# Longformer attention and a softplus feed-forward block on one core: global rows picked 512 columns at a time, the first q load cut by sequence, and the instruction order rebuilt

## The chip, the cores and the metric

The kernel runs on one core of one Trainium2 chip, in one launch. The metric is the device time in microseconds. A profiled execution gives the span from the first to the last instruction and the events inside it.

## The reference

The kernel fuses two functions. The first is attention with a window of 32 on both sides and eight global positions; the second is a feed-forward block with softplus.

```python
# q, k, v: [8 batches, 8 heads, 576 rows, 64]; global_idx: 8 rows
scores = (1 / np.sqrt(64)) * np.matmul(q, k.transpose(0, 1, 3, 2))
mask = np.abs(pos[:, None] - pos[None, :]) <= 32
mask = mask | is_global[:, None] | is_global[None, :]
attn = softmax(np.where(mask, scores, -1e9))
attn_out = np.matmul(attn, v)
x = attn_out.transpose(0, 2, 1, 3).reshape(8 * 576, 512)
h = x @ w_in                          # [4608, 512] @ [512, 2048]
g = np.maximum(h, 0.0) + np.log1p(np.exp(-np.abs(h)))
out = g @ w_out                       # [4608, 2048] @ [2048, 512]
```

## The kernel before

Each batch of 576 rows is cut into nine blocks of 64 rows; a unit is one such block with all eight heads, so there are 72 units. Four units are a group of 256 tokens, and two groups make a tile of 512 tokens for the feed-forward block; there are eight tiles.

Preparation of a batch (add_prep): one load brings q and one brings k (load_qk, L224), 72 partitions with eight sequence rows each, all heads. TensorE transposes them (tk L499, tq L507; 16 products of 72 columns for a pair of heads), and copies of ScalarE or VectorE put them into kx and qx. The rows of the eight global positions are picked by products with a 0/1 matrix pick_w (pick, L456): for each of q and k, eight products over the rows in a partition, for each of four pairs of heads, 128 columns each. Each pair of heads has its own quarter of the output's partitions. A copy (keep) brings the result to gk, a transposition (turn, L468) gives gt, and from there fill writes the global keys beside every window in kx, and gev writes the global queries to qg.

Scores of a unit come in two halves of four heads (sc, L621, and L626 in the first batch). VectorE adds the mask and finds the row's extreme (top, L632). ScalarE takes the exponentials (ex, L653). VectorE sums and inverts (su, L661 to L663). GpSimd scales: no (pn, L669) for the window and gc (gw, L673) for the global columns. The scaled block is transposed by TensorE (tp, L679) and copied (pt), or transposed by a DMA. The global rows have a part of their own: sg L548, gexp L561, tg L575, ov L586, oz L590. For four units together rt (L712) and val (xo, L734 and L744) give the attention output, which xev copies to xT.

The feed-forward block of a tile: first (h, L778) makes 16 groups of four products, soft (L784) takes softplus on ScalarE, second (o, L789) makes 16 products for each 128 tokens, and oev copies and stores. The first tile runs its first product in two halves of 256 tokens.

In the first batch q and k are loaded in two halves of four heads: k, q, then, after the constants are made, k, q again, all from GpSimd's queue. Blanks, the five loads of v and the two loads of w_in follow in that queue.

The order of all instructions is written out ahead of time by a planner in the kernel itself (class _Order). Each piece of work is added with a cost for each engine that can do it, its dependences, a rank, and the PSUM banks and buffers that it opens. run() takes, at each step, the piece that can start first, with the rank to break ties, and gives it to an engine. The engines then run their queues in that order. Ranks are shifted by two tables, OPENING for the early pieces and LATER for the others; KINDS says how many PSUM banks each kind of result may hold.

```python
    KINDS = dict(h=(4, 1), o=(2, 1), s=(2, 1), pick=(1, 2), gt=(1, 1), tk=(1, 2), tq=(4, 2), tk0=(2, 0), tq0=(2, 0),
                 sg=(2, 1), tg=(1, 0), ov=(1, 0), tp=(3, 0), rt=(3, 0), xo=(4, 2))
    OPENING = dict(ex=-1.5, gexp=-2, gsum=2.5, pt=2.5, softh=2, su=2, top=-2, w_out=-2)
    LATER = dict(blank_g=-1, blank_q=0.5, first=1, kev=-7, load=1, re=2, sg=2, soft=3, su=-0.5, tk=-5.5, tp=-1)
```

Of the kernel before, what the change touches and what calls it, by code (L numbers as in the profile page):

```python
# [18 lines left out]
class _Order:  # L19
# [15 lines left out]
    SWITCH = 95  # L35

# [41 lines left out]
    def run(self, free):  # L78
        waiting = {}
        after = {}  # L80
# [11 lines left out]
        while ready:  # L92
# [23 lines left out]
            step, took = j["cost"][e]  # L116
            for pool, key in j["opens"]:
# [9 lines left out]
            if e == "PE" and j["array"] != array:  # L127
                array = j["array"]
                t += self.SWITCH
            if j["moves"]:  # L130
# [24 lines left out]
def kernel(  # L155
# [71 lines left out]

    def load_v(b, t):
# [13 lines left out]
    load_qk(0, 0, 0, H // 2)  # L242
# [20 lines left out]
    for h in range(2):  # L263
# [3 lines left out]
    count(posA[:], [[P, NT5]], -WIN, 1)  # L267
    pick_w = const([P, QR, 32], BF16, "pick")
    clear(nc.vector, pick_w[:])
    nc.vector.tensor_tensor(out=pick_w[:, :, 0:NG], in0=posQ[:].unsqueeze(2).to_broadcast([P, QR, NG]),  # L270
                            in1=gf[:].unsqueeze(1).to_broadcast([P, QR, NG]), op=OP.is_equal)
# [22 lines left out]
    selg = const([P, 2, 2], FP32, "selg")  # L294
    hsel = temp([P, 2], FP32, "hsel")
# [5 lines left out]
    load_qk(0, 1, H // 2, H)  # L301
    load_qk(0, 0, H // 2, H)
# [56 lines left out]

    def select_rows():  # L360
# [17 lines left out]
    for c in range(KF):  # L378
        SLOTS[f"g{c}"] = 1

    KINDS = dict(h=(4, 1), o=(2, 1), s=(2, 1), pick=(1, 2), gt=(1, 1), tk=(1, 2), tq=(4, 2), tk0=(2, 0), tq0=(2, 0),
                 sg=(2, 1), tg=(1, 0), ov=(1, 0), tp=(3, 0), rt=(3, 0), xo=(4, 2))
# [24 lines left out]
    def pool(n):  # L407
        return {"POOL": (n, n)}
# [11 lines left out]
    def add_load(b, which, deps):  # L420
# [6 lines left out]
        early = [T.get(("t" + "qk"[which], b - 1, p)) for p in range(HP)]  # L427
# [12 lines left out]
    def add_prep(b, gate, rank):  # L440
# [8 lines left out]
        def pick(e, ws):  # L449
            if ("pick", b) not in PS:  # L450
                PS["pick", b] = psum(("pick", b), [P, 2, 2 * P], FP32)
                PS["gk", b] = sb.tile([P, 2, P], BF16, tag="gk", name="gk")
            for w in ws:
                for r in range(QR):
                    for p in range(HP):
                        nc.tensor.matmul(out=PS["pick", b][p * 32:(p + 1) * 32, w, 0:P], lhsT=pick_w[0:NQ, r, :],  # L456
                                         rhs=XN[w][0:NQ, p * 2:p * 2 + 2, r * D:(r + 1) * D],
                                         start=(r == 0), stop=(r == QR - 1))

        def keep(e, ws):  # L460
            r = slice(ws[0], ws[-1] + 1)
            copy(e, PS["gk", b][:, r, :], PS["pick", b][:, r, 0:P])

        def turn(e, ws):
            if ("gt", b) not in PS:
                PS["gt", b] = psum(("gt", b), [P, 2, HP, 32], BF16)
            for w in ws:
                nc.tensor.transpose(out=PS["gt", b][:, w, :, :], in_=PS["gk", b][:, w, :], identity=ident_b[:])  # L468
# [9 lines left out]
        steps = ((1,), (0,)) if b == 0 else ((0, 1),)  # L478
        for n, ws in enumerate(steps):
            T["pick", b, n] = o.add({"PE": (1040, 1160) if b == 0 else (460 * len(ws) + 190, 460 * len(ws) + 300)}, lambda e, ws=ws: pick(e, ws),  # L480
                                    [x for w in ws for x in T["load", b, w]] + [T.get(("pick", b, n - 1)), *gate], rank=4 if b or not n else 6, array=32,
                                    opens=[("pick", ("pick", b)), ("gk", ("gk", b))] if n == 0 else [],
                                    uses=[("pick", b), ("gk", b)])
# [51 lines left out]
        if b == 0:  # L535
            T["pick", 0, 1]["deps"] += [T["tq", 0, p] for p in range(2, HP)]
# [458 lines left out]
```

## Time and profile before

| | us |
|---|---|
| three runs, median (lowest to highest) | 375.19 (372.39 to 376.84) |
| profiled execution, its time | 370.3 |
| profiled execution, span of the core | 368.5 |
| TensorE busy | 342.6 (93%) |
| ScalarE busy | 277.5 (75%) |
| VectorE busy | 230.8 (63%) |
| GpSimd busy | 153.5 (42%) |

In the profile PE is TensorE's product, PEld its weight load, DVE is VectorE, ACT ScalarE, POOL GpSimd, SP SyncE. In the lists of instructions a line has the start and the time that it took in us, the engine, the source line, the operation, output and inputs, the shape, and a count; the bracket gives the idle time of the engine ahead of it and what ended it. "issue" means that the engine waited for nothing that the profile shows. Single products overlap, so the time per product is the distance of starts, not the time from start to end.

### The profile page before, as it was taken

What the parts mean: (1) busy time and instruction counts of PE and PEld (TensorE: products, weight loads), DVE (VectorE), ACT (ScalarE), POOL (GpSimd) and SP (SyncE); (2) the same over time, 40 slices, a digit from 0 to 9 for tenths busy, and PEclk for the clock granted to TensorE, in tenths of its full rate; (3) what the DMA queues carried; (4) which work ended last, traced back from release to release, by engine and by line L of the source; (5) the groups of instructions that cost most, each with busy time, mean ns of one, the idle gap of its engine ahead of it and who ended that gap; (6) DMA issues with size and microseconds to landing.
All of it is one profiled execution on the core that took longest, in us unless ns stands there. A gap on an engine that the chain in (4) does not pass through costs nothing.

```text
span 368.5 us, 11196 instructions
## 1 busy us (share of the span) xinstructions
PE 342.6 (93%) x4265; PEld 196.8 (53%) x4308; DVE 230.8 (63%) x1028; ACT 277.5 (75%) x709; POOL 153.5 (42%) x256
## 2 busy tenths in 40 slices
PE   2858999999999999899989999999999999999996
PEld 2646794565556454654464445554554455445444
DVE  5788796876588539854885568666965584163011
ACT  4598879986799679876978598859885996774710
POOL 8999712870079006910592049302930271050000
PEclk9999999999999999999999999999999999999999
DMA  6999993499049933993269516971691022021002
GB/s 92 171 221 162 179 216 57 99 97 189 15 116 136 184 65 98 123 202 64 86 117 174 106 46 133 165 142 45 129 138 45 31 86 59 0 74 59 0 29 85
DMA packets 86165, 39.01 MB, mean 106 GB/s; under 512 B 68064, under 2 KB 79584, under 8 KB 86112
## 3 DMA queue, kind: packets, MB, share of 16 engines
q0 software_dynamic: 53248, 18.37, 46.9%
q1 hardware_dynamic: 32864, 19.94, 22.2%
q8 instruction: 33, 0.54, 0.6%
q14 instruction: 20, 0.16, 0.1%
HBM read 36.71 MB, written 9.44 MB: 125 GB/s over the span
## 4 chain that ended last, share of the span: by engine, by line
PE 77%; DVE 10%; issue 4%; ACT 4%; POOL 3%; DMA 2%; DVEq 0%; POOLq 0%; ACTq 0%
PE h L778 33%; PE o L789 23%; PE s L621 4%; DVE sm L661 3%; PE xo L744 3%; PE pick L456 2%; PE tk L499 2%; PE tq L507 2%; PE tp L679 2%; DMA qn<-in_q_dram 2%; PE xo L734 2%; DVE st L632 2%; POOL pn L669 1%; ACT pe L653 1%; DVE rs L663 1%
## 5 line engine op out<-in xcount | busy, mean ns | idle before, releaser
L669 POOL TENSOR_TENSOR pn<-pe,rs 128x512 bf16<-128x512 f32 x72 | 74.8, 1039 | 173.2 <-DVE rs L663 136.2
L778 PE MATMUL h<-xT,win 128*128 128x512 bf16 (+1 forms) x625 | 135.8, 358 | 1.1 <-PE s L621 0.4
L789 PE MATMUL o<-wout,g 128*128 128x512 bf16 (+1 forms) x564 | 128.6, 373 | 2.0 <-issue 1.3
L784 ACT ACTIVATE g<-h 128x512 bf16<-128x512 f32 (+1 forms) x160 | 86.7, 555 | 45.5 <-PE h L778 44.4
L632 DVE CUSTOM_DVE_ANT_0 st<-s,mask 128x136 f32<-128x136 f32 x288 | 69.5, 296 | 47.7 <-PE s L621 45.0
L653 ACT ACTIVATE pe<-st,nb 128x136 f32<-128x136 f32 x288 | 92.5, 403 | 0.0
L778 PEld LDWEIGHTS <-win 128*128 128x128 bf16 x640 | 59.3, 98 | 50.5 <-issue 2.5
L789 PEld LDWEIGHTS <-g 128*128 128x128 bf16 x592 | 55.4, 98 | 55.4 <-DMA kn<-in_k_dram 0.3
L661 DVE TENSOR_REDUCE sm<-pe 128x4 f32<-128x544 f32 x63 | 44.7, 710 | 10.9 <-ACT pe L653 10.7
L231 POOL DMA_DIRECT2D vA<-in_v_dram x40 | 34.4, 875 | 0.0
L414 DVE COPY osb<-o 128x512 f32<-128x512 f32 (+1 forms) x21 | 13.8, 659 | 28.6 <-PE o L789 28.6
L621 PEld LDWEIGHTS <-qx 128*128 128x128 bf16 x252 | 20.6, 98 | 13.7
L621 PE MATMUL s<-kx,qx 128*128 128x136 bf16 x252 | 27.0, 223 | 0.4
L414 DVE COPY qx<-tq 64x576 bf16<-64x576 bf16 (+1 forms) x28 | 21.1, 753 | 4.7 <-PE tq L507 4.3
L632 DVE DVE_READ_ACCUMULATOR2_ANT nb<- 128x1 f32 x288 | 23.8, 83 | 0.0
L499 PE MATMUL tk<-ident_b,kn 72*64 72x72 bf16 x512 | 14.7, 207 | 7.6 <-DMA kn<-in_k_dram 7.3
L414 ACT COPY qx<-tq 64x576 bf16<-64x576 bf16 (+1 forms) x32 | 20.4, 637 | 0.9 <-PE tq L507 0.7
L663 DVE TENSOR_TENSOR rs<-rs,notg 128x4 f32<-128x4 f32 x72 | 17.7, 246 | 2.7 <-DVE rs L662 0.2
L414 ACT COPY kx<-tk 128x32 bf16<-128x32 bf16 (+1 forms) x63 | 15.9, 329 | 4.4 <-PE tk L499 4.3
L499 PEld LDWEIGHTS <-kn 72*64 72x64 bf16 x512 | 11.5, 118 | 11.7 <-DMA kn<-in_k_dram 7.5
L673 POOL TENSOR_TENSOR gw<-pe,rs 128x32 bf16<-128x32 f32 x72 | 16.8, 238 | 0.0
L662 DVE RECIPROCAL rs<-sm 128x4 f32<-128x4 f32 x72 | 12.7, 177 | 6.5
(110 smaller groups left out, 337.3 us busy)
## 6 DMA issues: line engine op xcount, KB each, us to landing
out_dram<-osb SPq DMA_DIRECT2D x35, 256.0 KB, 2.2
vB<-vA SPq DMA_DIRECT2D x16, 256.0 KB, 7.0
kn<-in_k_dram POOLq DMA_DIRECT2D x7, 576.0 KB, 12.5
qn<-in_q_dram POOLq DMA_DIRECT2D x7, 576.0 KB, 15.2
vA<-in_v_dram POOLq DMA_DIRECT2D x24, 128.0 KB, 6.1
win<-in_moe_w_in_dram POOLq DMA_DIRECT2D x2, 1024.0 KB, 13.8
wout<-in_moe_w_out_dram POOLq DMA_DIRECT2D x4, 512.0 KB, 10.2
vA<-in_v_dram POOLq DMA_DIRECT2D x16, 96.0 KB, 5.1
```

The costliest lines, as they stand in the source:

```text
L231: nc.gpsimd.dma_start(out=vA[b % 2][p0:p0 + hi - lo, t, :].rearrange("p (h d) -> p h d", h=H), in_=SRC[2][b, :, lo:hi, :].rearrange("h s d ...
L414: (nc.scalar.copy if e == "ACT" else nc.vector.tensor_copy)(out, in_)
L499: nc.tensor.transpose(out=ps[h * D:(h + 1) * D, r, :], in_=kn[0:NQ, p * 2 + h, r * D:(r + 1) * D], identity=ident_b[0:NQ, 0:NQ])
L621: nc.tensor.matmul(out=ps[:, y, :], lhsT=qx[i][:, p, j, :, :].rearrange("c h q -> c (h q)"), rhs=kf[:, p, j * W:j * W + EXT], start=True, ...
L632: nc.vector.tensor_tensor_reduce(out=PS["st", n][:, p, :], in0=PS["s", n, x][:, y, :], in1=mask[:, j, :], scale=-SCALE, scalar=3.0e38, op0 ...
L653: nc.scalar.activation(out=pe[:, p, 0:EXT], in_=PS["st", n][:, p, :], func=AF.Exp, bias=PS["nb", n][:, p:p + 1], scale=-1.0, **({"accum_ou ...
L661: nc.vector.reduce_sum(out=sm[:], in_=PS["pe", n][:, :, 0:EXT], axis=AX)
L663: nc.vector.tensor_tensor(out=rs[:], in0=rs[:], in1=notg[:, j:j + 1].to_broadcast([P, HP]), op=OP.mult)
L669: nc.gpsimd.tensor_tensor(out=pn[:].rearrange("c p (a s) -> c p a s", a=2), in0=wide[:, :, :, 0:G], in1=rs[:].unsqueeze(2).unsqueeze(3).to ...
L778: nc.tensor.matmul(out=h[:, :], lhsT=w_in_t[c * P // WC][:, kd, c * P % WC:c * P % WC + P], rhs=PS["xT", m][:, kd, lo:hi], start=(kd == 0) ...
L784: nc.scalar.activation(out=PS["g", m, c][:, lo:hi], in_=PS[key][:, :], func=AF.Softplus)
L789: nc.tensor.matmul(out=PS[key][:, :], lhsT=PS["g", m, kf][:, ns * P:(ns + 1) * P], rhs=w_out_t[kf // 4][:, kf % 4, lo:hi], start=(kf == 0) ...
```

## The change

It has four parts.

- The pick of a batch takes all eight heads in one product of 512 columns. The eight rows r of a partition are spread over the four quarters of the output's partitions (r and r + 4 accumulate), so there are eight products for q and eight for k in place of 64. The copy to gk is 512 columns for each of q and k, and the transposition becomes four products for each with sel8, a 0/1 matrix that adds up the four quarters; gt is f32 now. q and k are separate pieces in every batch.
- The first batch's k comes in two halves of heads, both ahead of the constants. Its q comes in two parts of the sequence, 32 and 40 of the 72 partitions, all heads: Q_PARTS puts the second at partition 64. Its transposes (tq and a new tqb), copies and pick are done part by part. pick_0 is a second 0/1 matrix for these places.
- The planner counts TensorE's instructions (many) and adds waits for the fetch of each 256; it doubles TensorE's costs until 3 us after the first values block.
- KINDS and the rank tables have new values, and a rank can be set for a single piece.

```diff
+    WARM = 3000
+    ASKS, HOLDS, COMES = 170, 448, 3600
...
+            if j.get("warms"):
+                self.cold = t + self.WARM
+            if e == "PE" and t < self.cold:
+                step, took = 2 * step, 2 * took
...
+            if e == "PE":
+                many = j.get("many", 2)
+                for x in range(issued, issued + many):
+                    if x % 256 == self.ASKS:
+                        block[x // 256] = t + (x - issued) * step / many + self.COMES
+                    if x % 256 == self.HOLDS % 256 and x >= self.HOLDS:
+                        late = block[(x - self.HOLDS) // 256] - (t + (x - issued) * step / many)
+                        step, took = step + max(0, late), took + max(0, late)
+                issued += many
...
+    Q_PARTS = ((0, 0, 32), (32, G, NQ - 32))
...
-    load_qk(0, 0, 0, H // 2)
+    load_qk(0, 1, H // 2, H)
...
-    load_qk(0, 1, H // 2, H)
-    load_qk(0, 0, H // 2, H)
+    for lo, at, n in Q_PARTS:
+        nc.gpsimd.dma_start(out=qn[at:at + n, :, :],
+                            in_=q[0].rearrange("h (q r) d -> q h (r d)", r=QR)[lo:lo + n])
...
+    def make_sel8():
+        sel8f = temp([P, NG], FP32, "sel8f")
+        nc.vector.reduce_sum(out=sel8f[:], in_=ident[:].rearrange("p (a r) -> p r a", r=32)[:, 0:NG, :], axis=AX)
+        nc.vector.tensor_copy(sel8[:], sel8f[:])
...
-    KINDS = dict(h=(4, 1), o=(2, 1), s=(2, 1), pick=(1, 2), gt=(1, 1), tk=(1, 2), tq=(4, 2), tk0=(2, 0), tq0=(2, 0),
-                 sg=(2, 1), tg=(1, 0), ov=(1, 0), tp=(3, 0), rt=(3, 0), xo=(4, 2))
+    KINDS = dict(h=(4, 2), o=(3, 1), s=(2, 0), pick=(2, 0), gt=(1, 2), tk=(4, 0), tq=(4, 2), tk0=(1, 0), tq0=(2, 0),
+                 sg=(2, 1), tg=(2, 1), ov=(1, 1), tp=(2, 0), rt=(3, 0), xo=(4, 1))
...
-        def pick(e, ws):
...
-            for w in ws:
+            ps = PS["pick", b, w] = psum(("pick", b, w), [P, H, D], FP32)
+            parts = ((pick_w, 0, NQ),) if b or w else tuple((pick_0, at, n) for lo, at, n in Q_PARTS)
+            for z, (pw, at, n) in enumerate(parts):
                 for r in range(QR):
-                    for p in range(HP):
-                        nc.tensor.matmul(out=PS["pick", b][p * 32:(p + 1) * 32, w, 0:P], lhsT=pick_w[0:NQ, r, :],
-                                         rhs=XN[w][0:NQ, p * 2:p * 2 + 2, r * D:(r + 1) * D],
-                                         start=(r == 0), stop=(r == QR - 1))
+                    c = r % 4 * 32
+                    nc.tensor.matmul(out=ps[c:c + 32, :, :], lhsT=pw[at:at + n, r, :],
+                                     rhs=XN[w][at:at + n, :, r * D:(r + 1) * D],
+                                     start=(r < 4 and z == 0), stop=(r > 3 and z == len(parts) - 1))
...
-                nc.tensor.transpose(out=PS["gt", b][:, w, :, :], in_=PS["gk", b][:, w, :], identity=ident_b[:])
+            for p in range(HP):
+                nc.tensor.matmul(out=PS["gt", b][:, w, p, :], lhsT=PS["gk", b][:, w, p * P:(p + 1) * P], rhs=sel8[:, :],
+                                 start=True, stop=True)
...
-        steps = ((1,), (0,)) if b == 0 else ((0, 1),)
+        for n, w in enumerate((1, 0)):
...
+            def tq(e, z=0, p=p, parts=parts):
+                lo, at, n = parts[z]
+                ps = PS["tq", b, p, z] = psum(("tq", b, p, z), [P, QR, n], BF16)
                 for r in range(QR):
                     for h in range(2):
                         nc.tensor.transpose(out=ps[h * D:(h + 1) * D, r, :],
-                                            in_=qn[0:NQ, p * 2 + h, r * D:(r + 1) * D],
-                                            identity=ident_b[0:NQ, 0:NQ])
+                                            in_=qn[at:at + n, p * 2 + h, r * D:(r + 1) * D],
+                                            identity=ident_b[at:at + n, at:at + n])
...
-    OPENING = dict(ex=-1.5, gexp=-2, gsum=2.5, pt=2.5, softh=2, su=2, top=-2, w_out=-2)
-    LATER = dict(blank_g=-1, blank_q=0.5, first=1, kev=-7, load=1, re=2, sg=2, soft=3, su=-0.5, tk=-5.5, tp=-1)
+    OPENING = dict(blank_w=-2, first=0.5, no=0.5, oev=2, ones_g=-2, sec=4.5, su=2.5, w_in=1, w_out=-4)
+    LATER = dict(first=2, gc=-1, kev=-8, oev=-0.5, pick=2, qev=1, re=2, sec=1, sg=3, su=1.5, top=-0.5, w_out=-4)
```

The resulting order of the opening differs as follows. TensorE takes a k group, the k pick, k, two q groups of the first part, gt, k, two more q groups, the first halves of units 0 and 1, k, two q groups of the second part, the first halves of units 2 and 3, the last two q groups, the second half of unit 0, the q pick, and then the other scores. On GpSimd the four loads of w_out go ahead of pn of units 5 to 8, gw goes ahead of pn in the first eight units, and the two memsets of the mask's ends come behind the five loads of v. On ScalarE the copies pt of units 4 and 5 stand between the exponentials of units 6, 7 and 8. In later batches q and k transposes, the two picks and the values block stand in another order, and the first tile's scores of batch 1 come in the second half of its h groups instead of through both.

## The prediction

> **What bounds the kernel now.** I read the table of busy time in four stretches first, because the whole-span shares mix a start-up with a long steady part.
>
> ```profile
> core 0: us, PE busy (x) PEld busy (x) DVE busy (x) ACT busy (x) POOL busy (x), PEclk, DMA share, GB/s
> ...
> 16.30:34.00 17.70, 12.39 (x172) 8.79 (x169) 15.79 (x102) 15.99 (x78) 16.07 (x33) 1.00 1.11 201
> 34.00:368.50 334.50, 322.06 (x3888) 181.20 (x3929) 205.61 (x882) 254.35 (x613) 122.85 (x186) 1.00 0.65 100
> ```
>
> The first long product (h, L778) starts at 34.00. From there TensorE is busy 322.1 of 334.5 us while VectorE (DVE) has 61% and ScalarE (ACT) 76%. So after 34 only TensorE work and TensorE gaps count. Between 16.3 and 34, ACT, DVE and POOL are all at about 90% and TensorE is not: the chain of exponentials (L653) sets the time there.
>
> Then the timeline of TensorE around the global-row products (pick, L456):
>
> ```profile
> 39.98 1.21 PE L507 MATMUL tq<-ident_b,qn 72*64 72x72 bf16 x64
> 41.02 0.43 PE L499 MATMUL tk<-ident_b,kn 72*64 72x72 bf16 x16
> 41.38 0.51 PE L456 MATMUL pick<-qn,pick 72*32 72x128 bf16 x21
> 42.69 0.35 PE L456 MATMUL pick<-qn,pick 72*32 72x128 bf16 x11 [0.80 <-issue]
> ```
>
> A run of equal products stops for 0.80 us with nothing that releases it ("issue"). Such stops stand at instructions 1210, 2234, 4278, 5046, 5300, 6068 and 7088 of TensorE's order: 176 to 186 past a multiple of 256, each time. The queue table explains the 256:
>
> ```profile
> q8 instruction: 33, 0.54, 0.6%
> ```
>
> 33 packets of 16 KB carry TensorE's 8618 instructions, 256 each. TensorE ran out of instructions. Start to start, less the normal spacing, the seven cost 1.0 + 0.56 + 0.74 + 0.99 + 0.53 + 0.60 + 0.50 = 4.9 us. The 0.25 us "issue" ahead of most other picks is not such a stop: the order has a 512-column product (0.22 us) there which the trace did not record.
>
> Last the opening, TensorE and ACT:
>
> ```profile
> 8.19 1.17 PE L507 MATMUL tq<-ident_b,qn 72*64 72x72 bf16 x32 [0.52 <-DMA qn<-in_q_dram]
> 10.18 1.17 PE L499 MATMUL tk<-ident_b,kn 72*64 72x72 bf16 x32 [0.82 <-DMA kn<-in_k_dram]
> 11.28 1.04 PE L456 MATMUL pick<-kn,pick 72*32 72x128 bf16 x32
> 12.62 1.17 PE L507 MATMUL tq<-ident_b,qn 72*64 72x72 bf16 x32 [0.29 <-DMA qn<-in_q_dram]
> ```
>
> ```profile
> 16.28 0.41 ACT L653 ACTIVATE pe<-st,nb 128x136 f32<-128x136 f32 x1
> ...
> 33.26 1.14 ACT L414 COPY pt<-tp 128x512 bf16<-128x512 bf16 x2 [1.69 <-PE tp L679]
> 34.42 1.28 ACT L784 ACT_TABLE_LOAD   x1
> 35.71 0.38 ACT L784 ACTIVATE g<-h 128x256 bf16<-128x256 f32 x1
> ```
>
> The reader sees when the four loads land (6.5, 8.2, 10.2, 12.6) and that 32 transposes take 1.10 here (10.18 to 11.28) but 64 take 1.04 at 40: TensorE runs at half rate before 34, though the granted-clock column says 1.00. Exponentials start at 16.28; softplus starts at 35.71 and frees the h banks.
>
> **The change, part by part, from 368.5 us of span.**
>
> *Instructions.* Pick goes from 64 to 16 products per batch, each with its weight load: 96 fewer, 768 in eight batches. The second transposition of the picked rows (gt, L468) grows from 2 to 8 products, and the first batch has 64 more transposes and 8 more pick products. 8618 becomes 8090. I added row prices along both orders, from 170 past a multiple of 256 to the need 272 later. In the old order this gives 2.4 to 2.9 us at five of the seven stops, 3.6 at 41.9, over 5 at 195.7 (its packet came late, behind another stop), and 3.1 at one place that did not stop. In the new order the shortest spans after the opening are 3.4, 3.5, 3.5, 3.6, 3.7 and 4.3. At the short stops the instructions were there 3.2 to 3.6 us after the asking place, so I take 4.9 - 0.2 = 4.7 us saved. Bounds: 4.9 saved, and 0.7 lost if every fetch takes the 4.6 us of the one at 41.9 (1.2 + 1.1 + 1.1 + 1.0 + 0.9 + 0.3 = 5.6 us of stops instead of 4.9).
>
> The Trainium skill, Runtime: NRT & Kernel Launch, section Instruction fetch mechanics, also has 16 KiB blocks of 256 instructions, but says that the fetch is hidden because issue is slower than refill. By that the stops have another cause and nothing of the 4.7 is sure; the seven places above speak against it.
>
> *Pick products.* Old: 227.63 to 228.64, 1.01 us for 64. New: four rounds of 512 columns; the eight sg products (L548; 384 and 256 columns, four column places at once) took 0.39 with one 0.1 change of array shape, 0.45 ns a column, so 2048 columns make 0.92 + 0.1. Gain 0 to 0.04 a batch; I take 0.3 in all, with one array change less here and there.
>
> *Eight gt products.* Width 8, weights 128 wide. Bounds from rows: 16 ns each (L744, 64-wide weights) and 59 (L621, 128-wide, 136 columns). They keep the wide weights and lose the columns, so 45: 0.36 - 0.11 = +0.25 a batch, +1.7 us in the seven later batches (0 to +2.5).
>
> *Copies.* Two of 128x512 f32 (0.58 on ACT, 0.68 on DVE, row xT<-xo) replace one of 0.42, and the fill reads f32: some 0.9 us a batch, behind the 322 us of TensorE. Costed at nothing; without that cover, 6 us.
>
> *Opening.* The second half of k takes the place of the first half of q in POOL's queue (landing 8.2). The first part of q (32 of 72 rows, all heads) leaves where the second k half did, after two more short iotas: about 10.3. The rest follows 2.2 to 2.9 later. Queued behind these two issues are the blanks and the v loads, as before; the two mask memsets now wait behind five v issues (4.2 us), to about 12.3, ahead of the first score. What TensorE must do from 10.3 until the first unit has all heads: two k groups (0.55 each), eight q groups, gt (0.4), five score groups (0.26, from 15.72 to 16.77 for four) and seven array changes (0.12). A q group now has 32 or 40 columns: 0.25 to 0.3 if columns set it, 0.55 if its 64-wide weights do. 5.8 to 8.2 us, so 16.1 to 18.5, and with the two top steps the first exponential at 16.8 to 19.2. The 64-column products at 31.62 took 1.00 for 32, nearly the price of 72 columns, so I lean up: 17.8, 1.5 late. TensorE waits for the last q load in none of this.
>
> Then nine units at 1.57 and the global one at 0.97; unit 1 waits 0.6 for its second half, which stands behind the q pick (1.9 at half rate). Two pt copies (0.57) now stand between units. POOL issues four w_out loads (0.75 to 0.83) ahead of the products pn of units 5 to 7; unit 8's exponentials stand on ACT behind the copy of unit 5, hence behind that pn (about 33.6). So: copy 34.8, unit 8 to 36.4, table, softplus at 37.7, 2.0 late. On TensorE the second values block, four k groups and a pick of batch 1 fill that wait; the fifth h group starts at about 40.0. At 40.0 the old order had done eight h groups and three k groups; the new one four h, four k and a pick: 4 x 0.44 - 0.36 - 0.55 = 0.8 us behind. Bounds from the two ends of the first exponential: 0.7 ahead, 2.5 behind.
>
> The Trainium skill, TensorE: Matmul & The Clock Gate, What's actually happening, has the clock open after about 3.4 us of sustained work. The trace disagrees: 11.28 to 18.54 is nearly gapless and stays at half rate. In the new opening TensorE is dense from about 10.3; the rule alone would make that a rival, below.
>
> *Everything else:* 4 us of other waits after 34 and the 3 us after the last product stay.
>
> Sum: -4.7 + 1.7 - 0.3 + 0.8 = -2.5: span 366.0, its time 370.3 - 2.5 = 367.8. The three runs have a median of 375.19, 1.3% over the profiled time, so 372.6 there.
>
> **Rivals.**
> 1. The opening as columns price it: first exponential 16.8, 0.7 ahead, and gt at 30 ns, below the middle of its bounds (+0.9). -4.7 + 0.9 - 0.3 - 0.7 = -4.8; 365.5 x 1.013 = 370.3. For it: nothing shows what 32 columns cost. Against: the 64-column row. 0.25.
> 2. The clock opens early: with TensorE dense from 10.3, the work left from some 14 on (4 us until the first exponential) runs at the full rate and ACT starts 2 us sooner: -2.5 - 2.0, 370.6. Against: the dense stretch above. 0.05.
> 3. The stops are not of the instruction count, or the same number return: -2.5 + 4.7 = +2.2, 377.4. 0.10.
> 4. Slower: fetches take 4.6 us, as at 41.9, in the six short spans, because each falls among loads and transposes by DMA: 5.6 us of stops instead of 4.9. 0.7 + 1.7 - 0.3 + 0.8 = +2.9, 378.1. It is slower than before once a fetch takes over 4.1. For: the 41.9 packet left 2.1 us after asking. Against: four others were there after 3.2 to 3.4. 0.14.
>
> The forecast has 0.46.
>
> **How the numbers follow.** About 1% (3.8 us) is what a measurement of this kernel tells from no change. Faster by more (under 371.4): 0.21 from rivals 1 and 2 and a third of the forecast, 0.36. Slower by more (over 378.9): 0.06 of rival 4, 0.02 of rival 3, and 0.05 of the forecast's upper tail, with the first exponential at 19.2 and waits for the copies added. Within: 0.51. The range 366.5 to 379 takes in all the cases with their own spread; the forecast's own is 369.5 to 376.
>
> **What would show it.** Right: no "issue" gap over 0.2 us in a run of small products after 40; 31 packets in the instruction queue; pick x16 in about 1.0 us; eight gt in 0.3 to 0.45; first exponential near 17.8, softplus near 37.7, fifth h group near 40. Wrong: a stop of 0.5 us or more 176 to 186 past a multiple of 256; 16 short q transposes well under 0.4; softplus before 36; a TensorE gap for gk, kx or qx in later batches.

## The result, and the profile after

Over 22 timed runs each, the changed kernel has a median of 371.74 us and the kernel before 373.66. The ratio is 0.9948 with a 95% interval of 0.9925 to 0.9972: 1.9 us faster, half a per cent. One of the changed kernel's 22 runs took 595.41 us at a mean granted clock of 0.58 and one 377.11; the medians take in all runs, the ratio leaves these two out. In a second series the ratio is 0.9939 (0.9908 to 0.9970).

The two profiled executions say something else. The changed kernel took 371.55 us with a span of 369.8; before took 370.3 with 368.5. Over one execution each, the changed kernel lost 1.3 us. Both statements have to be explained.

The same stretches as in the prediction, for the changed kernel (columns: busy time and instructions of PE, PEld, DVE, ACT, POOL; granted clock; DMA share; GB/s):

```profile
16.30:34.00 17.70, 14.17 (x198) 8.13 (x193) 15.58 (x90) 14.64 (x70) 14.50 (x28) 1.00 1.21 214
34.00:369.80 335.80, 328.13 (x3653) 179.71 (x3651) 214.16 (x891) 254.98 (x636) 124.44 (x188) 1.00 0.67 99
```

TensorE is still what bounds the kernel after 34. ScalarE is busy 14.6 us between 16.3 and 34, where it was 16.0: the chain of exponentials now has holes.

What TensorE waited for (total, times, longest; the lines that matter here):

```profile
PE tp L720 <- POOL pn L710: 2.8, 5, 0.9
...
PE tq L544 <- issue: 0.9, 1, 0.9
PE tq L544 <- DMA qn<-in_q_dram: 0.7, 1, 0.7
PE xo L785 <- DMA pt<-pn: 0.5, 1, 0.5
```

and its instruction queue:

```profile
q8 instruction: 31, 0.51, 0.6%
```

31 packets in place of 33. One instruction stop of size is left, 0.9 us in the q transposes at 82.89: it stands at instruction 2228, 180 past a multiple of 256. A second of 0.4 us (start to start) is at 2994, 178 past.

The opening, TensorE (x lines are runs of equal products):

```profile
9.96 1.03 PE L544 MATMUL tq<-ident_b,qn 32*64 32x32 bf16 x32
...
14.68 0.88 PE L544 MATMUL tq<-ident_b,qn 40*64 40x40 bf16 x26 [0.68 <-DMA qn<-in_q_dram]
...
17.20 2.01 PE L491 MATMUL pick<-qn,pick 32*32 32x512 bf16 x16
...
43.19 1.47 PE L819 MATMUL h<-xT,win 128*128 128x256 bf16 x12
44.71 0.26 PE L502 MATMUL gt<-sel,gk 128*128 128x8 bf16 x4
```

ScalarE:

```profile
16.96 0.41 ACT L694 ACTIVATE pe<-st,nb 128x136 f32<-128x136 f32 x1
...
36.59 0.58 ACT L448 COPY pt<-tp 128x512 bf16<-128x512 bf16 x1 [2.46 <-PE tp L720]
...
40.06 0.38 ACT L825 ACTIVATE g<-h 128x256 bf16<-128x256 f32 x1
```

POOL:

```profile
31.22 0.83 POOL L878 DMA_DIRECT2D wout<-in_moe_w_out_dram  x1
...
32.26 1.55 POOL L878 DMA_DIRECT2D wout<-in_moe_w_out_dram  x2
...
34.01 0.80 POOL L878 DMA_DIRECT2D wout<-in_moe_w_out_dram  x1
34.84 2.04 POOL L710 TENSOR_TENSOR pn<-pe,rs 128x512 bf16<-128x512 f32 x2
```

The reader sees a chain: VectorE has unit 5's factor ready at 31.3, but four w_out issues, 3.2 us of POOL's time, come before its product pn at 34.84; the transposition and ScalarE's copy at 36.59 wait for that product; unit 8's exponentials stand behind the copy, and softplus, which frees the h banks, comes at 40.06 where it was 35.71.

TensorE's own speed differs too. The same eight products of 256 columns, first in before, then in the changed kernel:

```profile
34.00 1.10 PE L778 MATMUL h<-xT,win 128*128 128x256 bf16 x8
```

```profile
36.35 1.91 PE L819 MATMUL h<-xT,win 128*128 128x256 bf16 x8
```

Before has 109 ns a product from 34.2 on. The changed kernel has 213 ns until 39.0 and 109 behind that: it runs at half rate for 4.9 us longer, and the granted-clock column (1.00) doesn't show it. Ahead of these products TensorE stood idle for 0.9 us, up to 35.95, waiting for pn of unit 5.

I added the row prices of the prediction along both kernels' TensorE orders (gt at 30 ns) and compared them with the trace. The difference between clock time and priced work, taken at 43 us and added to all the priced work, is when TensorE would finish if it lost nothing more: 356.4 us for before (ahead of its first stop), 360.8 for the changed kernel, so 4.4 lost. From there on before loses another 8.6 us, 4.9 of them in its seven stops; the changed kernel loses 5.5, of which 1.5 in two stops. 4.4 - 3.1 = 1.3, the difference of the spans.

### The profile page after: what moved, and what is told of

It reads as the page before. It is cut to its first block, busy times and chain, and to the rows that moved or that the text cites. A ratio compares the mean times of both kernels' runs of the same rounds, so it can differ in the third digit from the quotient of the medians.

```text
span 369.8 us, 10736 instructions
## 1 busy us (share of the span) xinstructions
PE 350.3 (95%) x4044; PEld 194.3 (53%) x4044; DVE 239.5 (65%) x1028; ACT 277.2 (75%) x724; POOL 153.4 (41%) x258
## 4 chain that ended last, share of the span: by engine, by line
PE 68%; DVE 15%; ACT 7%; DMA 4%; issue 3%; POOL 3%; DVEq 0%; POOLq 0%; ACTq 0%
PE h L819 34%; PE o L830 16%; DVE sm L702 6%; PE s L662 4%; PE xo L785 3%; ACT pe L694 2%; PE tq L544 2%; DMA qn<-in_q_dram 2%; DVE rs L704 2%; PE pick L491 2%; DVE rs L703 2%; PE tk L533 2%; DVE osb L448 2%; PE xo L775 1%; ACT L602 1%
## 5 line engine op out<-in xcount | busy, mean ns | idle before, releaser
L819 PE MATMUL h<-xT,win 128*128 128x512 bf16 (+1 forms) x640 | 138.8, 361 | 0.1
L830 PE MATMUL o<-wout,g 128*128 128x512 bf16 (+1 forms) x592 | 136.2, 374 | 0.0
L819 PEld LDWEIGHTS <-win 128*128 128x128 bf16 x640 | 60.1, 99 | 50.9 <-issue 2.0
L448 DVE COPY osb<-o 128x512 f32<-128x512 f32 (+1 forms) x26 | 17.3, 664 | 28.2 <-PE o L830 28.1
L448 DVE COPY qx<-tq 64x576 bf16<-64x576 bf16 (+2 forms) x35 | 25.5, 728 | 5.6 <-PE tq L544 5.0
L448 ACT CAST xT<-xo 128x512 bf16<-128x512 f32 x19 | 10.9, 590 | 12.1 <-PE xo L785 12.1
L533 PE MATMUL tk<-ident_b,kn 72*64 72x72 bf16 x512 | 13.5, 205 | 6.2 <-DMA kn<-in_k_dram 6.2
L448 ACT COPY kx<-tk 128x32 bf16<-128x32 bf16 (+1 forms) x75 | 18.0, 359 | 1.9 <-PE tk L533 1.8
L704 DVE TENSOR_TENSOR rs<-rs,notg 128x4 f32<-128x4 f32 x72 | 17.7, 246 | 2.5
L448 ACT COPY qx<-tq 64x576 bf16<-64x576 bf16 (+2 forms) x29 | 17.2, 593 | 1.9 <-PE tq L544 1.6
## 6 DMA issues: line engine op xcount, KB each, us to landing
qn<-in_q_dram POOLq DMA_DIRECT2D x7, 576.0 KB, 14.6
```

What stands on the lines that cost most here:

```text
L448: (nc.scalar.copy if e == "ACT" else nc.vector.tensor_copy)(out, in_)
L533: nc.tensor.transpose(out=ps[h * D:(h + 1) * D, r, :], in_=kn[0:NQ, p * 2 + h, r * D:(r + 1) * D], identity=ident_b[0:NQ, 0:NQ])
L704: nc.vector.tensor_tensor(out=rs[:], in0=rs[:], in1=notg[:, j:j + 1].to_broadcast([P, HP]), op=OP.mult)
L819: nc.tensor.matmul(out=h[:, :], lhsT=w_in_t[c * P // WC][:, kd, c * P % WC:c * P % WC + P], rhs=PS["xT", m][:, kd, lo:hi], start=(kd == 0) ...
L830: nc.tensor.matmul(out=PS[key][:, :], lhsT=PS["g", m, kf][:, ns * P:(ns + 1) * P], rhs=w_out_t[kf // 4][:, kf % 4, lo:hi], start=(kf == 0) ...
```

## The experiments

### A second profile of each kernel

Both unchanged. Expected of before:

> The kernel before, unchanged, for a second profile. The first one took 370.3 us where the median of its timed runs is 373.7, and the profiled execution of the changed kernel 371.55 where its median is 371.7. Theory: the first profile was an unusually quick execution, and a second one lies at 371 to 375, with the difference in waits that vary from run to run (loads by DMA, instruction fetches). Rival: profiled executions of this kernel are always about 1% quicker than timed ones: 369 to 371 again.

Measured: 372.33 us, span 370.0. Six of the seven stops stand at the same instructions (1210, 2234, 5046, 5300, 6068 and 7088), two of them longer and one shorter. The one at 4278 is missing; just ahead of its place TensorE waits 1.7 us for a pt transposed by DMA, a wait that the first profile does not show:

```profile
PE pick L456 <- issue: 2.9, 7, 1.2
...
PE xo L744 <- DMA pt<-pn: 1.7, 1, 1.7
```

Of 98 timed runs of before in all comparisons none is under 371.3. The profile on which the prediction's sum stood (370.3) was an unusually quick execution, as the theory says. The second one lies where the theory put it, but still at the quick end of the 19 timed runs beside it (372.30 to 377.92), so it isn't excluded that profiles of this kernel tend to come out quick. Against a usual execution the changed kernel is ahead.

Of the changed kernel:

> The changed kernel unchanged, for a second profile on the same chip as the next three kernels. Nothing is in dispute here but what varies: the 0.9 us instruction stop at 82.9 should stand at the same instruction (2228), softplus within 0.3 of 40.06, and the wait for a transposed pt near 121 (0.5 in the first trace, 1.3 to 1.7 in other kernels) may differ. Theory: TensorE runs at half its granted clock for some 6 us where that wait passes about 1.3 us and not where it is 0.5, so that runs of 374 and more are those with the longer wait. Rival: the clock dips without any wait ahead of it.

Measured: median 371.28 us; the execution that was profiled took 376.57. Its stop at instruction 2228 lasts 1.6 us, and the pt wait 1.2 (start to start). Behind each of the two the granted clock is halved for 3.4 us; the first:

```profile
82.00:84.00 2.00, 0.56 (x33) 0.41 (x26) 1.73 (x3) 1.56 (x3) 2.00 (x4) 1.00 2.92 71
84.00:86.00 2.00, 1.69 (x27) 1.24 (x28) 1.51 (x2) 1.08 (x4) 0.91 (x2) 0.54 2.42 153
86.00:88.00 2.00, 2.00 (x8) 0.70 (x6) 0.00 (x0) 1.97 (x3) 0.62 (x1) 0.61 1.91 163
88.00:90.00 2.00, 2.00 (x15) 1.06 (x14) 1.56 (x9) 1.38 (x3) 0.00 (x0) 1.00 1.19 174
```

The third column from the right is the granted clock. The stop ends at 83.95; of 84 to 88 some 3.4 us run at half rate, which costs 1.7 us more. So a stop can cost twice its length, and this has its own experiment below. Both dips have a wait ahead of them, so the rival is out here; but 1.2 was enough, and the spells were shorter than the theory's 6 us.

The timed runs say something of how much of the gain hangs on such spells. In this series 8 of the 35 runs of before and 9 of the 10 of the changed kernel have a mean granted clock of 0.998 or more. Their medians are 372.5 and 371.2 us, 1.3 apart, where all runs together are 2.2 apart (373.44 and 371.28). The other 0.9 goes with executions at a lower mean clock, of which before has more. Which of these had such a spell, and which only show the opening at half rate (see the last section), the means do not tell.

### Do the stops follow the count?

```
 ahead of the first batch's pick of k:
+    for x in range(24):
+        nc.tensor.matmul(out=ps[0:32, 0, 0:32], lhsT=ident_b[0:NQ, 0:32],
+                         rhs=ident_b[0:NQ, 0:32], start=True, stop=True)
```

> The changed kernel with 24 small products more (48 instructions) ahead of the first pick, where TensorE waits 1.22 us for k anyway; every later instruction is counted 48 further on. Theory (TensorE stops where it is 448 instructions past the place that asks for the next 256 and has come there in less than about 3.4 us): in the trace of the changed kernel these 272 instructions, counted 48 earlier, take 2.41 us at one place and 2.76 at another, so a stop of 1.0 us stands near instruction 3002 and one of 0.6 near 4794, perhaps 0.2 to 1.0 near 2234, all 176 to 186 past a multiple of 256; 0.8 to 1.7 us slower than the changed kernel. Rival (the stops belong to the work, or to the transfers that go on beside it): the 0.9 us stop stays in the same run of q transposes, now at 2276, and no other appears; the time is the changed kernel's within 0.3 us.

Measured: median 374.30, ratio to before 1.0004 (0.9972 to 1.0036), where the changed kernel has 0.9948: some 2 us slower, a little over the forecast. In the profiled execution a pt wait of 1.3 us that ends at 120.4 goes over into 6.8 us at half clock, which the forecast did not have. Nothing stands at 2276, where the work of the old stop now is. A stop of 0.65 us (start to start) is at 2228 again, 180 past, where other products now are; one of 0.5 is at 6572, 172 past. At 4784, 176 past, a pick breaks off for 1.2 us:

```profile
197.11 0.62 PE L494 MATMUL pick<-qn,pick 72*32 72x512 bf16 x8 [0.81 <-ACT kx L448]
```

The profile puts this one down to a copy on ScalarE which ended at about 196.7; the instructions' packet left at 194.83, and the stop ended 3.5 us after TensorE passed the asking place. The instructions fit: in before's seven stops the stop ended 2.2 to 2.7 us after the packet left, here 2.3, and the copy had been over for 0.4 us. That the copy had a share isn't excluded. The stop forecast at 3002 did not come: its packet had left at 111.10, 2.5 us before TensorE came to the place that I took for the asking one. The count is of what the queue takes in, and where a wait stands before that, the queue is ahead of the products; my price of the span was too short there.

What follows: the stops belong to the count and not to the work. How long a span is cannot be read from products alone.

This trace also shows what the late full rate costs. GpSimd's queue, the wait for pn of unit 5 (0.98 us) and softplus (39.88) are nearly as in the changed kernel, but the eight products behind the wait, at 36.2, already take 109 ns each, and the fifth h group starts at 42.40, 0.8 us ahead of 43.19.

### The parts of the change

The pick alone in the kernel before:

```
-  16 x 4 products of 128 columns, two gt transposes
+  for r in range(QR):                                  # 8 products of 512 columns each for q and k
+      nc.tensor.matmul(out=ps[c:c + 32, :, :], lhsT=pw[at:at + n, r, :], ...)
+  eight gt products against sel8
   (loads, ranks, bank shares and the planner of before)
```

> The kernel before with only the pick over 512 columns, its copies, and the eight gt products; loads, ranks and bank shares are those of before, and the order is made without instruction fetches. By the row prices of TensorE along its order: +3.3 us of work against before (array changes 11.74 us instead of 9.12, gt 1.0, pick -0.3); of the seven stops (4.9 us) at most 0.2 is left by the count, since its order is 672 instructions shorter and only two spans of 272 instructions fall under 3.4 us (3.37 and 3.23). Sum -1.4: ratio to before about 0.996. Rival (the stops are not of the count): they stay, and it is 3 us slower than before, ratio about 1.009.

Measured: 371.87 us, ratio 0.9926 (0.9899 to 0.9953). Its longest "issue" wait in a run of small products is 0.3 us; by row prices at most 0.5 is lost at one place (3766, 182 past). The seven stops are gone and the rival is out, and the new pick alone is worth as much as the whole change, within the intervals. The gain is larger than the forecast of 0.996; why, these runs do not show.

The other side, the changed kernel with the old tables:

```
-    KINDS = dict(h=(4, 2), o=(3, 1), s=(2, 0), pick=(2, 0), ...)
+    KINDS = dict(h=(4, 1), o=(2, 1), s=(2, 1), pick=(1, 2), ...)
     OPENING, LATER, BOUND as before
```

> The changed kernel with the ranks and bank shares of before. Row prices along TensorE's order give +3.6 us against the changed kernel (array changes 12.42 us instead of 8.83); no span of 272 instructions is under 3.7 us, so its one stop of 0.9 goes. In the opening only one w_out load is issued ahead of the products pn of units 7 and 8, none ahead of 5 and 6. Theory (those issues cost about 2 us of the changed kernel's opening): softplus before 39 instead of 40.06, and 3.6 - 0.9 - 2 = 0.7 us slower than the changed kernel, ratio to before about 0.997. Rival (the opening's loss is the q load in sequence parts): softplus stays near 40, 2.7 slower than the changed kernel, ratio about 1.002. Second rival (array changes cost less than 0.097 us where the next loads are ready): ratio about 0.99.

Measured: 375.04 us, ratio 1.0007 (0.9969 to 1.0044); softplus at 36.93. The opening's loss goes with the tables, as the theory has it: with w_out behind pn of units 5 and 6, softplus is 3.1 earlier although q still comes in sequence parts. The time is about 2 us over the changed kernel's, not 0.7: a pt wait of 1.4 us (start to start) near 119.7 is followed by 3.4 us at half clock (1.7 us), which no row price holds. Most of the 3.6 us of array changes come from the bank shares alone: with the new KINDS and the old ranks the same prices give 9.0 us of them along the order (counted along the planned order, not run). The planner's instruction-fetch term was not tried by itself.

### The opening: w_out, and q in parts

```
 order = o.run(...)
+the four T["w_out", a] taken out, and put in behind T["no", 7]
```

> The changed kernel with one thing moved: the four w_out loads are issued by POOL behind the product pn of unit 7, not ahead of those of units 5 to 7; every other engine's order is the same. Theory (the opening's loss is that queue): pn of unit 5 starts at about 33.0 instead of 34.84, its copy on ScalarE at 34.7 instead of 36.59, softplus at 38.0 to 38.5 instead of 40.06, the fifth h group at about 41.4 instead of 43.19, and the time is 1.5 to 2 us less than the changed kernel's: ratio to before about 0.990. Rival (unit 8 or the late q is what the copies wait for): softplus stays over 39.5 and the time within 0.5 us of the changed kernel. If the w_out loads are then late for the first second-layer products, TensorE shows a wait on wout after 45.

Measured: softplus at 38.51 and pn of unit 5 at 33.02, both as the theory said. The time is 373.47, ratio 1.0009 (0.9975 to 1.0044): slower than the changed kernel by 2 us. POOL and TensorE show why:

```profile
36.40 3.07 POOL L878 DMA_DIRECT2D wout<-in_moe_w_out_dram  x4
39.43 1.80 POOL L251 DMA_DIRECT2D vA<-in_v_dram  x2
41.20 0.29 POOL L714 TENSOR_TENSOR gw<-pe,rs 128x32 bf16<-128x32 f32 x1
41.40 1.08 POOL L710 TENSOR_TENSOR pn<-pe,rs 128x512 bf16<-128x512 f32 x1
```

```profile
42.54 0.61 PE L720 MATMUL tp<-ident_b,pn 128*128 128x128 bf16 x4 [2.50 <-POOL pn L710]
```

```profile
42.00:44.00 2.00, 1.46 (x9) 1.17 (x10) 0.81 (x2) 0.00 (x0) 2.00 (x3) 0.50 1.04 161
44.00:46.00 2.00, 2.00 (x15) 1.47 (x13) 1.39 (x7) 1.02 (x3) 1.81 (x7) 0.50 1.21 199
46.00:48.00 2.00, 2.00 (x12) 1.40 (x10) 0.33 (x1) 0.90 (x3) 1.78 (x4) 0.50 1.23 205
```

No wait on wout shows. The loads now stand ahead of unit 8's pn, which TensorE needs next. The stall moved by one unit, and the stop of 2.5 us halved the clock for 6.8 us.

q as two head halves, w_out left in place:

```
-    Q_PARTS = ((0, 0, 32), (32, G, NQ - 32))      # by rows, 32 and 40, all heads
+    load_qk(0, 0, 0, H // 2); load_qk(0, 0, H // 2, H)
+    one pick over 72 rows, one group of 16 transposes for each pair of heads
```

> The changed kernel with the first batch's q loaded and transposed as two head halves behind the two k halves, and its pick made once over 72 rows: 64 transposes and 8 pick products fewer, 144 instructions. Ranks and bank shares as in the changed kernel; the order is planned anew, and the w_out loads stay ahead of pn. Theory (queue on POOL): first exponential earlier, 15.8 to 16.8, but softplus still at 39 to 40.5. Rival (the q in sequence parts is what the opening lost): softplus at 37 to 38 and fifth h group at 40 to 41. By row prices 2.1 us of TensorE's work go (half of it before 34), and the count puts one span of 272 instructions at 2.56 us near instruction 6330, so one stop of about 0.85: by the theory the time is within 1 us of the changed kernel, by the rival 2 less.

Measured: first exponential at 15.73, softplus at 36.80, and 372.54 us, 0.9986 (0.9948 to 1.0023), no faster than the changed kernel. Softplus is where the rival had it, so the parts of q have a share too. The stop forecast near 6330 did not come. The fifth h group comes at 45.92 all the same: a stop of 1.9 us (start to start) ends at 43.21 at instruction 952, 184 past a multiple of 256, and the clock is halved behind it. The instructions were asked for about 36.5, and their packet left at 40.98. In between GpSimd issued v loads, and the DMA engines were busy in every slice from 36 to 44; that the one delayed the other isn't shown.

> q as head halves and the w_out loads behind pn of unit 7. Theory: the two add up only in the part that POOL's queue held: first exponential 15.8 to 16.8, softplus at 37 to 38, fifth h group at 40 to 41, the stop near instruction 6330 as in the kernel with head halves alone; ratio to before about 0.988. Rival (softplus is bound by the nine units of exponentials, 1.57 each, and the two copies between them): softplus no earlier than with the w_out move alone.

Measured: first exponential 16.31, softplus 37.38, and 374.00 us, ratio 1.0004 (0.9970 to 1.0037) in place of 0.988. TensorE stopped 2.7 us ahead of unit 8's transposition at 42.22, as with the w_out move alone, and the clock was halved for 10.2 us. The stop near 6330 did not come here either.

Then the same move one unit further, behind T["no", 8]:

> The changed kernel with the four w_out loads issued behind the product pn of unit 8 (the kernel before this one in the list put them behind unit 7, and then TensorE waited 2.5 us for pn of unit 8 at 42.5 and ran at half its granted clock from 41.7 to 48.1). Theory (the opening's loss is POOL's queue, and that stop gave it back): softplus at 38.5, pn of unit 8 at 38.4 instead of 41.40, no TensorE wait over 0.5 us and no half clock between 38 and 60, fifth h group at 40.2 to 40.8 instead of 43.19, 2 to 2.7 us less than the changed kernel: ratio to before about 0.988. Rival (the next thing in POOL's queue, the v loads of the second batch, takes its place): TensorE waits for them or for pn again, fifth h group not before 42, time as the changed kernel's.

Measured: median 369.80, ratio 0.9874 (0.9824 to 0.9924). Softplus and the fifth h group:

```profile
38.88 0.38 ACT L825 ACTIVATE g<-h 128x256 bf16<-128x256 f32 x1
```

```profile
41.18 1.47 PE L819 MATMUL h<-xT,win 128*128 128x256 bf16 x12 [0.34 <-DVE kx L448]
```

No TensorE wait over 0.34 from 38 to 60, and no half clock there. The fifth h group is 0.4 later than forecast. Two of the 4.4 us went with the move: finishing time with nothing more lost is 358.8, against 360.8. They are not the queue alone. Here TensorE has its full rate from 34.8 on. The kernel shifted by 48 has the old queue and the full rate by 36.2, and its fifth h group is at 42.40; from there the move gains 1.2, and the other 0.8 is the half rate up to 39.0. Whether that half rate follows from the wait for pn of unit 5 is open: of the four profiles with this wait (the changed kernel's two, the shifted one and the one with 16 stops) three reach the full rate at 39.0 to 39.8 and one by 36.2.

The rest of the opening:

```
 q as head halves, w_out behind T["no", 8]
+12 small products ahead of the first pick
```

> The changed kernel with the first batch's q as two head halves (its pick once, over 72 rows), the four w_out loads issued behind the product pn of unit 8, and 12 small products (24 instructions) ahead of the first pick, which move the places where TensorE needs its next 256 instructions out of the short spans (shortest left by rows: 3.3, 3.35, 3.38). What it tells apart: how much of the opening's loss is left once w_out is out of the way. Theory (q in sequence parts has a share of its own of about 2 us: 64 more transposes and 8 more picks at half rate): softplus at 36.8 to 37.8 where the w_out move alone has 38.88, 1 to 2 us less than that kernel, 367.8 to 368.8, ratio to before 0.982. Rival (the w_out queue was all that mattered, the rest of the opening is bound by exponentials): softplus within 0.4 of 38.88 and the time within 0.5 us of the w_out move alone, ratio 0.987.

Measured: first exponential 15.78, softplus 36.83, as the theory had it; 369.00 us, ratio 0.9898 (0.9871 to 0.9925). By the finishing time with nothing more lost it is 1.1 better than the w_out move alone (357.7 against 358.8). By the comparison with before it is not: the interval overlaps that of the w_out move. One stop of 1.0 us is at instruction 3762, 178 past. The share of q's parts in the time is not settled.

### What a stop costs

```
 if m and c in (3, 11):                       # tiles 2 to 9, two places in each
+    nc.vector.tensor_copy(wide[:, 0:P], h[:, 0:P])     # or straight into mark, with no POOL work
+    n times: nc.gpsimd.tensor_tensor(out=wide[:], in0=wide[:], in1=wide[:], op=OP.subtract)
+    nc.gpsimd.tensor_tensor(out=mark[:], ...)
 ahead of the next h group:
+    nc.tensor.matmul(out=h[:, 0:P], lhsT=mark[:], rhs=mark[:], start=True, stop=True)
```

> The changed kernel with 16 stops put into its dense stretches: in tiles 2 to 9, ahead of the fifth and the thirteenth h group, TensorE waits for a product's copy on VectorE and 0 to 2 long operations of POOL behind it; stops of some 0.5, 1.8 and 2.8 us. The output is the reference's. Theory (a stop itself halves the clock): the granted clock falls to 0.50 for 3 to 6.5 us after most of the stops over 1.2 us and after none under 1.0, so each of those costs 1.6 to 3.3 us more than itself. Rival (the halving belongs to the batch borders, to narrow transposes and loads there): none of the 16 stops is followed by it and the kernel loses their sum alone.

Measured, in a single run: 403.50 us, with six stops up to 0.5, six of 2.0 and four of 3.1 (idle time). The clock falls behind two of the four longest alone; one of 2.0 and one of 3.1, and what follows each:

```profile
99.17 0.23 PE L823 MATMUL h<-mark 128*128 128x128 bf16 x1 [1.98 <-POOL mark L833]
...
141.14 0.23 PE L823 MATMUL h<-mark 128*128 128x128 bf16 x1 [3.10 <-POOL mark L833]
```

```profile
99.00:101.00 2.00, 1.83 (x13) 1.01 (x14) 0.58 (x5) 0.60 (x1) 0.12 (x1) 1.00 0.03 8
101.00:103.00 2.00, 2.00 (x14) 1.06 (x13) 1.00 (x9) 1.19 (x2) 0.00 (x0) 1.00 0.00 0
...
142.00:144.00 2.00, 2.00 (x9) 1.02 (x8) 0.97 (x8) 0.60 (x1) 0.00 (x0) 0.50 0.00 0
144.00:145.00 1.00, 1.00 (x4) 0.33 (x3) 0.00 (x0) 0.21 (x1) 0.00 (x0) 0.50 0.00 0
```

Both theories fall in part. A stop by itself can halve the clock in the dense part, but only at 3.1 us, and then not always; six of 2.0 did nothing. At the batch borders, among transposes and 64-column products, 1.0 to 1.8 us of idle time were enough in six cases (the second profile of the changed kernel, twice; those shifted by 48, with the old tables, with q as head halves, and with w_out behind unit 8), while 1.2 and 1.7 us in the second profile of before did nothing.

### A version that beats both

```
 before + the new pick + KINDS, OPENING and LATER of the changed kernel
-    OPENING = dict(..., w_out=-4)
+    OPENING = dict(..., w_out=0)
+    12 small products ahead of the first pick
```

> The kernel before with the pick over 512 columns, the bank shares and ranks of the changed kernel but for w_out (rank 0 in the opening in place of -4), its own four loads in the old order, and 12 small products (24 instructions) ahead of the first pick, chosen so that no span of 272 instructions is under 3.35 us by row prices. Work of TensorE by rows 335.0 us, where the pick alone has 338.1 and before 334.8 (array changes 8.5 us against 11.7 and 9.1). Theory (gain = stops gone, the bank shares keep the array changes down, and the old opening loses nothing): opening as with the pick alone (softplus at 36 to 37), no instruction stop over 0.3 us, 3 us less than the pick alone: 368 to 369.5, ratio to before about 0.986. Rival (array changes cost nothing where ScalarE or a bank is what the next group waits for): as the pick alone, 0.992.

Measured: 368.79 us, ratio 0.9838 (0.9799 to 0.9877). One break of 1.1 us (idle time) is left at 3768, 184 past, which the profile puts down to a copy. Against the pick alone the ratio is 0.9 per cent lower, 3.3 us; the rows took off 3.1 us of work (338.1 to 335.0, nearly all array changes). The tables change more than the array changes, so this match alone doesn't prove their price. The rows of the changed kernel do: a 512-column product is followed after 0.216 us by one of the same array shape and after 0.31 by one of another, 0.09 to 0.10 a change. The rival, that array changes are free, is out.

## Why the prediction was right, and where it was not

372.6 us was forecast, 0.7% below the median; 371.74, 0.5% below its median, was measured. The amount is right. The working is right on the stops and wrong on the opening, and that the two medians still agree is in good part luck, as the last paragraph shows.

*Instruction stops, -4.7.* The mechanism holds: pick alone removes all seven, and shifted instructions bring stops back near 178 past 256. The size was 3.4 (4.9 to 1.5). The span at 2234, priced 3.5 us, stopped because its packet left 2.0 us after the asking place and came 4.3 us after it: rival 4's slow fetch. At the second stop, 2994, they came 3.8 us after it. So two of the six short spans stopped, and one of the prediction's own signs of being wrong, a stop of 0.5 us or more 176 to 186 past a multiple of 256, was there once. Rival 3 is refuted.

*Eight gt products, +1.7.* 25 to 30 ns each (four in 0.12 us), not 45: at most +0.9. What sets this price no run shows.

*Pick, -0.3.* Held: 54.5 ns a product, 0.87 us for 16, 0.98 with the change of array shape where the old 64 took 1.01. The array changes that it could bring were not priced beyond one less here and there, and this is luck: with the old bank shares they are 2.6 to 3.3 us more than in before. With the new ones they are 0.3 less.

*The opening, +0.8, bounds 0.7 ahead and 2.5 behind.* This is the step that failed: 4.1 (4.4 less 0.3 of work in later batches), outside its bounds. The first exponential came earlier than I said (16.96, not 17.8), and q's first part a little sooner than forecast (9.96). The second half of q landed late, and TensorE did wait 0.7 for it. The price of short transposes was right at the upper end (32 in 0.97). The miss lies behind that: I had pn of unit 5 at about 33.6 and its copy at 34.8; pn began at 34.84 and the copy at 36.59. VectorE's factor of unit 7 began at 34.53 and ended only at 35.92, with that same pn, so the top step of unit 8's scores came no sooner either. Softplus at 40.06 in place of 37.7 and the fifth h group at 43.19 in place of 40.0 follow. I named the four issues ahead of pn and priced the chain behind them 2 us too short; moving them gave 2.0 us back. I also priced TensorE at full rate from 34, where the trace has half rate up to 39.0. By the kernel shifted by 48 that is 0.8 us of the fifth h group's 3.2, and it is in the 2.0. Rival 2, a full rate that comes early, did not happen: it came 4.9 us later than in before.

*Copies, nothing.* Held: no TensorE wait for gk, kx or qx over 0.4.

*Against the profile's own time* the sum gave -2.5 and the profiles +1.3: the terms of the sum, measured, do not give the forecast. That the medians agree with it is luck. The sum stood on a quick execution of before and was scaled to a median; in that median before also pays for stops and pt waits that vary, and for halved clocks, and the sum had none of these. They made up for the opening.

## What to carry to other kernels

Where one engine runs for the whole span, count its instructions: a rewrite that leaves its busy time as it was can still be worth most of a per cent (0.7 with the pick alone) by taking small products out of a dense stretch. After any change of an order made by a planner, price the array changes along the new order; here they are worth more than the change itself. A load that is issued early on an engine which also computes must be placed behind the last product that something waits for, and one unit too early only moves the stall.

## What the runs showed of the hardware

*Half clock behind a stop.* Behind a stop the spells last 3.4, 6.8 or, once, 10.2 us (q as head halves with w_out behind unit 7), and cost half of the time that TensorE works in them. The Trainium skill, TensorE: Matmul & The Clock Gate, What's actually happening, has a free-running window of 3413 ns; the lengths agree. Its advice in Why this matters for your kernels, no idle gaps over about 3 us, fits the dense part (two of four at 3.1, none of six at 2.0) and not the batch borders, where 1.0 us was enough.

*The granted clock of the opening.* TensorE's opening runs at half rate in every profile, with 1.00 in the column, so its rate has to be read from the products: 213 ns for 256 columns at half rate, 109 at full. Only the profile of the best version shows it in the column:

```profile
24.00:30.00 6.00, 3.90 (x48) 2.42 (x48) 5.80 (x34) 5.97 (x30) 5.06 (x7) 0.50 1.15 206
30.00:36.00 6.00, 4.42 (x61) 3.41 (x62) 4.68 (x21) 4.92 (x20) 5.76 (x10) 0.50 1.47 164
```

*VectorE held by POOL.* A small operation of VectorE with two SBUF inputs that meets a pn on GpSimd ends with that pn:

```profile
27.21 1.67 DVE L610 SCALAR_TENSOR_TENSOR rv<-selg,rv 128x2 f32<-128x2 f32 x1
```

```profile
27.82 1.04 POOL L710 TENSOR_TENSOR pn<-pe,rs 128x512 bf16<-128x512 f32 x1
```

27.21 + 1.67 = 28.88 and 27.82 + 1.04 = 28.86; the first takes 0.2 where no pn runs. This one began 0.6 us ahead of pn; the one at 60.88 in before began 0.13 us into a pn of 1.03 and took 0.92. In the first profile of the changed kernel and the second of before, 35 of 36 and 32 of 33 such operations (L704, L608 and L610, in before L663, L567 and L569) that started within a pn, or saw one start, ended 0.02 to 0.03 us behind it. The other two began less than 0.1 us ahead of its end and took their usual 0.16. The Trainium skill, GPSIMD Engine Reference, Specifications, names this contention for two SBUF inputs; the trace agrees and gives its size, up to nearly all of a pn that runs.
